# The head of an attention-and-Mish kernel reordered, one copy moved to ScalarE, and four output stores moved behind an activation

## The chip, the cores and the metric

One core of a Trainium2 chip runs the kernel. The metric is the device time of one execution in microseconds (us): the median of several runs, and for one of them a profile. The engines are PE (TensorE, matmuls), DVE (VectorE), ACT (ScalarE), POOL (GpSimd) and SP (SyncE, which only issues transfers here). ACT and POOL issue transfers as well, in line with their other work. The inputs are float32; the kernel works in float16 and accumulates in float32 in PSUM, the memory that PE writes and that DVE and ACT read.

## The reference

A causal linear attention with decay, per batch entry and head, and then two matrix products with an activation between them. B = 4, H = 8, S = 768, D = 64; w_in is 512 x 2048 and w_out 2048 x 512.

```python
Dmask = where(rel >= 0, lam ** rel, 0)           # within a block
for each block b of the sequence:
    intra = (einsum('bhic,bhjc->bhij', qb, kb) * Dmask) @ vb
    inter = einsum('bhid,bhde->bhie', qb * lam ** (pos + 1), kv_state)
    out[block] = intra + inter
    kv_state = lam ** block * kv_state + (kb * rev_pow)^T @ vb
x = out as (B*S) x (H*D)
h = x @ w_in
g = h * tanh(softplus(h))                        # Mish
result = g @ w_out
```

## The kernel before

The sequence is cut into NG = 6 groups n of C = 128 positions; with B = 4 batch entries a group has four chunks of 128 rows. Chunk c = 4 n + b is one batch entry's 128 positions, all eight heads. For the chunks of groups 0 and 1, one chunk goes through these steps:

- `first_t(c)` (L246): PE transposes k into PSUM tile `pk`, ACT copies it to `pkT` (L237); PE transposes q into `pq`, DVE copies it to `pqT` (L242 in group 0). In group 0 the q of chunks 1 to 3 is laid out differently, so its transposes are 16 small matmuls (L222).
- `first_s(c)` (L269): `scores` (L253) multiplies pkT and pqT on PE into two PSUM tiles `pS`, 8 matmuls (L260). `masks(c, 0)` and `masks(c, 1)` (L264) multiply each tile by the decay mask on DVE, giving two tiles `sb`.
- `first_o(c)` (L294): `outputs` (L274) multiplies sb with v into PSUM tile `pO` on PE; `copy_out` (L290) copies it on ACT into `xt`, the transposed attention output of the group. There is one PSUM buffer each for pk, pq and pO, so outputs of a chunk wait for copy_out of the chunk before.

Then the dense part: `mm1_unit(n, u)` (L424) is four matmuls of 512 columns (L421) that make 128 of the 2048 hidden columns in PSUM tile `ph` (two buffers), and one Mish on ACT into `hsg` (L428). `mm2_unit` multiplies hsg with w_out into `po` (L453); after the last part of a batch entry `mm2_out` (L460) copies po on ACT to `osb` (L462 calls L468) and issues the store on ACT's queue (L465). For later groups k and q are transposed by DMA (`turn`), and their scores and outputs are placed between the dense units.

The order of each engine's work is the order of the program text (a manual schedule); each engine runs its own instructions strictly in that order and waits on semaphores for the others. `busy(m)` (L172) issues m matmuls of zeros, 512 columns each, into a tile that nobody reads. `clear(b)` sets a part of the state `wst` to zero on DVE; `scale_k` (L301) makes `ktil`, the decayed k, on DVE for group 0 and on POOL for group 1. The loads of k, q, v and the weights are issued by POOL; w_in arrives in pieces, in this order: two of 128 columns, one of 256, three of 512 columns.

The program text around the change: the head is L492 to L538 (chunks 0 to 3, with `mm1_part` computing the first 384 columns of units 0 and 1 ahead of the last chunk). L557 to L568 run the 16 units of group 0 and place chunk 4's and 5's steps behind units 11 to 15. The loop at L584 runs the rest: for n = 1 the output units of groups 0 and 1, from n = 2 on the 16 units of group n and its output units.

Of the kernel before, what the change touches and what calls it, by code (L numbers as in the profile page):

```python
# [9 lines left out]
AF = mybir.ActivationFunctionType  # L10
# [3 lines left out]
def bc(ap, axis, n):  # L14
    shape = list(ap.shape)
    shape.insert(axis, n)
    return ap.unsqueeze(axis).broadcast_to(shape)
# [3 lines left out]
def kernel(  # L21
# [10 lines left out]
    nc = tc.nc  # L32
    B, H, S, D = q.shape
    C = 128
    NG = S // C
# [136 lines left out]
    def busy(m):  # L172

        t = ps.tile([128, 4 * C], F32, name="busy", tag="ph", bufs=2)
        for _ in range(m):
            nc.tensor.matmul(t, kzero, kzero2, start=True, stop=True)  # L176
# [38 lines left out]
    def turn_pe(c, name):  # L215

        src = (k0 if c == 0 else kn[c] if c < B else ktil[c]) if name == "pk" else (q0 if c == 0 else qn[c])
        if 0 < c < B and name == "pq":
            pt = ps.tile([128, JP, C], F32, name=name, tag=name)
            for r in range(RS):  # L220
                for x in range(2):
                    nc.tensor.matmul(  # L222
                        pt[64 * x : 64 * x + 64].rearrange("p j (s r) -> p j s r", r=RS)[:, :, :, r],
                        src[:, r, :], own[:, :, x, :], start=True, stop=True)
        else:
            pt = ps.tile([128, JP, C], F16, name=name, tag=name)
            for j in range(JP):
                nc.tensor.matmul(  # L228
                    pt[:, j, :], src[:, 2 * j : 2 * j + 2, :].rearrange("p h c -> p (h c)"), ident,
                    is_transpose=True, start=(j == 0), stop=(j == JP - 1),  # L230
                )
        kq[c, name] = work.tile([128, JP, C], F16, name=f"{name}T", tag=f"{name}T", bufs=2)
        return kq[c, name], pt

    def first_k(c):
        to, pt = turn_pe(c, "pk")
        nc.scalar.activation(to, pt, AF.Copy)  # L237

    def first_q(c):
        to, pt = turn_pe(c, "pq")  # L240
        if c < B:
            nc.vector.tensor_copy(to, pt)  # L242
        else:
            nc.vector.tensor_tensor(out=to, in0=pt, in1=lq, op=ALU.mult)

    def first_t(c):  # L246
        first_k(c)
        first_q(c)
# [4 lines left out]
    def scores(c):  # L253

        kT, qT = kq[c, "pk"], kq[c, "pq"]
        pS = [ps.tile([128, JP, C], F32, name="pS", tag=("pS", "po")[t], bufs=1 + t) for t in range(2)]
        for j in range(JP):
            for t in range(2):
                rs = slice(64 * t, 64 * t + 64)
                nc.tensor.matmul(pS[t][:, j, :], kT[rs, j, :], qT[rs, j, :], start=True, stop=True)  # L260
        score[c] = pS
        sb0[c] = [None, None]

    def masks(c, t):  # L264
        sb0[c][t] = work.tile([128, JP, C], F16, name="sb", tag="sb", bufs=4)
        nc.vector.tensor_tensor(out=sb0[c][t], in0=score[c][t],  # L266
                                in1=dm[:, t] if c < B else bc(maskT, 1, JP), op=ALU.mult)

    def first_s(c):  # L269
        scores(c)  # L270
        masks(c, 0)
        masks(c, 1)

    def outputs(c):  # L274
        n, b = divmod(c, B)
        if xt[n] is None:
            xt[n] = work.tile([128, JP, GT], F16, name="xt", tag="xt", bufs=2)
        psO = ps.tile([128, JP, C], F32, name="pO", tag="pO")
        vf = vz[c].rearrange("p h c -> p (h c)")
        for j in range(JP):  # L280
            if n:
                nc.tensor.matmul(psO[:, j, :], wst[:, b, j, :],
                                 kq[c, "pq"][:, j, :], start=True, stop=False)
            for t in range(2):
                o = 4 * D * j + D * t
                nc.tensor.matmul(psO[:, j, :], vf[:, o : o + 128], sb0[c][t][:, j, :],  # L286
                                 start=(n == 0 and t == 0), stop=(t == 1))
        outs[c] = psO

    def copy_out(c):  # L290
        n, b = divmod(c, B)
        nc.scalar.activation(xt[n][:, :, b * C : (b + 1) * C], outs[c], AF.Copy)  # L292

    def first_o(c):  # L294
        outputs(c)
        copy_out(c)
# [4 lines left out]
    def scale_k(i):  # L301

        t = work.tile([128, H, D], F16, name="ktil", tag="ktil", bufs=8)
        (nc.vector if i < B or i >= (NG - 1) * B else nc.gpsimd).tensor_tensor(  # L304
            out=t, in0=kn[i], in1=bc(lk, 2, D), op=ALU.mult)
        ktil[i] = t
# [101 lines left out]
    def behind(src):  # L408
        nc.gpsimd.tensor_copy(tick, src)  # L409
# [46 lines left out]
                )  # L456

    last_out = [None]

    def mm2_out(n, b, po, lo, hi, copy, queue):  # L460
        osb = work.tile([128, hi - lo], F32, name="osb", tag=f"osb{hi - lo}", bufs=3)
        copy(osb, po[:, lo:hi])  # L462
        last_out[0] = osb
        r0 = b * S + n * C
        queue.dma_start(out=out[r0 : r0 + C, lo:hi], in_=osb)  # L465

    def act_copy(o, i):
        nc.scalar.activation(o, i, AF.Copy)  # L468
# [20 lines left out]
    def clear(b):  # L489
        nc.vector.memset(wst[:, b], 0.0)  # L490
# [14 lines left out]
    nc.scalar.activation(lbc, lnp, AF.Exp, scale=float(C))  # L505
    q_decays()
    busy(1)
    scores(0)
    masks(0, 0)
    first_t(1)  # L510
    masks(0, 1)
    nc.scalar.preload_act_table(AF.Mish)
    busy(1)
    scores(1)
    masks(1, 0)
    outputs(0)
    first_t(2)
    copy_out(0)
    masks(1, 1)
    busy(2)  # L520
    first_s(2)
    first_o(1)
    clear(1)
    busy(2)
    first_t(3)
    clear(2)
    busy(2)
    first_s(3)
    first_o(2)
    busy(2)  # L530
    mm1_part(0, 0, 0, GT - C)
    first_o(3)
    mm1_part(0, 1, 0, GT - C)
    scale_k(0)
    scale_k(1)
    clear(3)
    scale_k(2)
    scale_k(3)  # L538
# [15 lines left out]
    load_wout(3)  # L554
    load_k(2 * B)
    load_q(2 * B)
    steps = {11: ((first_t, 4),), 13: ((first_s, 4),), 14: ((first_t, 5),), 15: ((first_o, 4), (first_s, 5))}  # L557
    for u in range(NKI):
        mm1_unit(0, u)
        if u in (1, 3):  # L560
# [9 lines left out]
    for c in (g + 1, g + 2, g + 3):  # L570
        load_k(c)
        load_q(c)
    steps = {(4, 0): ((first_t, 6),), (4, 1): ((first_o, 5), (first_s, 6)), (4, 2): ((first_t, 7),),
             (4, 3): ((first_o, 6), (first_s, 7)), (5, 1): ((first_o, 7),),
             (6, 1): ((state_half, 0), (turn, g)), (6, 2): ((state_half, 1),)}
# [8 lines left out]
    for n in range(NT - 1, NG):  # L584
        dense = [(mm2_unit, m, b, part) for m in ((0, 1) if n < NT else (n,))
                 for b in range(B) for part in range(WS)]
        if n >= NT:
            dense = [(mm1_unit, n, ni) for ni in range(NKI)] + dense
        todo = {}

        def at(u, f, *args):
            todo.setdefault(u, []).append((f, args))

        if n + 1 < NG:
            pairs = []
            for b in (0, 2):
                s = Pair()
                s.n, s.b = n + 1, b
                pairs.append(s)
            steps = (((9, pair_s, 0), (13, pair_o, 0), (16, pair_s, 1), (20, pair_o, 1),  # L600
                      (24, pair_a, 1)) if n < NT else
                     ((4, pair_s, 0), (8, pair_o, 0), (13, pair_s, 1), (17, pair_o, 1),
                      (20, pair_a, 1)))
            for u, f, b in steps:
                at(u, f, pairs[b])
        if n == NT:
            at(0, lambda: behind(hsg[n][0:1, 0, 0:1]))
            at(0, turn, (n + 1) * B + 2)
            at(0, turn, (n + 1) * B + 3)
        if n + 2 < NG:  # L610
            c = (n + 2) * B
            loads_ = [(f, c + b) for b in range(B) for f in (load_k, load_q)]
            loads_ += [(load_v, c + b) for b in range(B)]
            for x, (f, i) in enumerate(loads_):
                if n >= NT:
                    u = (1, 2, 3, 5, 6, 8, 10, 11, 12, 13, 14, 15)[x]
                    at(u, lambda u=u: behind(hsg[n][0:1, u, 0:1]))
                else:
                    u = 7 + x // 2 * 4
                    if x % 2 == 0:  # L620
                        at(u, lambda: behind(last_out[0][0:1, 0:1]))
                at(u, f, i)
            for b, u in enumerate((21, 23) if n < NT else (18, 19, 21, 23)):
                at(u, turn, c + b)
        for u, (fn, *args) in enumerate(dense):
            fn(*args)
            for f2, args in todo.get(u, ()):
                if args and isinstance(args[0], Pair):
                    args[0].spare = "po" if u < NKI - 1 and n >= NT else "ph"
                f2(*args)  # L630
# [30 lines left out]
```

## Time and profile before

| | |
|---|---|
| median of 3 runs | 211.84 us (211.42 to 212.21) |
| the profiled execution | 212.23 us, of which 210.4 us span from the first to the last instruction |
| PE busy | 204.0 us, 97% of the span |
| ACT busy | 86.5 us, 41% |
| DVE busy | 68.3 us, 32% |
| POOL busy | 98.8 us, 47% |
| L453 (second product) | 400 matmuls, 85.4 us |
| L421 (first product) | 328 matmuls, 73.2 us |
| L176 (`busy`) | 16 matmuls, 6.8 us |

How to read it: busy time counts a matmul from its start to its modelled end, and neighbours overlap, so 97% does not mean that PE does useful work all that time; the filler of L176 counts as busy too. A timeline row gives the start, the time from the first start to the last end of a run of like instructions, the engine (with a q where its sequencer issues a transfer), line, operation, output and inputs, shapes, the count, and in brackets the idle time of the engine before it and what ended it.

### The profile page before, as it was taken

Reading aid. Unit: us, or ns where it says so; the run is one execution under the profiler, and the core shown is the slowest. Engines: PE = TensorE matmul, PEld = TensorE weight load, DVE = VectorE, ACT = ScalarE, POOL = GpSimd, SP = SyncE. Lnnn points to the kernel's source line nnn. Section 1 sums busy time; section 2 is a strip of 40 time slices with the busy share of each in tenths; the row PEclk is TensorE's granted clock in tenths of the full one; section 3 lists DMA queues with packets and bytes.
Section 4 is the critical chain, followed back from the end, with each engine's and each line's share of the span. In section 5 each row is a group of like instructions: output and inputs, shape, how many; then the busy total and the mean of one; then the engine's idle time right before and its main releaser. Section 6 shows DMA issues by size and latency. Waiting matters only on the chain.

```text
span 210.4 us, 4359 instructions
## 1 busy us (share of the span) xinstructions
PE 204.0 (97%) x1794; PEld 111.0 (53%) x1794; DVE 68.3 (32%) x124; ACT 86.5 (41%) x150; POOL 98.8 (47%) x143
## 2 busy tenths in 40 slices
PE   7998999999999999999999999999999999999993
PEld 4556446999745554454544445544455544444452
DVE  7578715525004632042540042681042600000000
ACT  4944576665421112356312456212456221666120
POOL 7997299934964558796874176840000000000000
PEclk9999999999999999999999999999999999999999
DMA  8999999999999999999996799996802042100112
GB/s 123 146 166 200 182 152 98 189 188 158 135 181 189 196 131 170 204 169 151 134 152 161 197 78 94 138 160 149 189 3 50 2 103 101 50 0 0 53 50 100
DMA packets 107591, 26.78 MB, mean 127 GB/s; under 512 B 99890, under 2 KB 104626, under 8 KB 107570
## 3 DMA queue, kind: packets, MB, share of 16 engines
q0 software_dynamic: 75776, 13.38, 83.1%
q1 hardware_dynamic: 27296, 6.63, 20.8%
q10 hardware_dynamic: 4498, 6.49, 10.0%
q8 instruction: 14, 0.23, 0.5%
q14 instruction: 7, 0.06, 0.1%
HBM read 27.26 MB, written 6.29 MB: 159 GB/s over the span
## 4 chain that ended last, share of the span: by engine, by line
PE 94%; DMA 2%; DVE 1%; ACT 1%; issue 0%
PE po L453 40%; PE ph L421 34%; PE ph L439 7%; PE pS L365 2%; PE pO L286 2%; PE pO L392 2%; DMA kn<-in_k_dram 2%; PE pv L329 1%; PE pS L260 1%; DVE pqT L242 1%; PE pk L228 1%; PE pq L222 1%; PE pO L371 1%; PE pq L228 1%; PE busy L176 1%; ACT xt L292 1%
## 5 line engine op out<-in xcount | busy, mean ns | idle before, releaser
L453 PE MATMUL po<-wout,hsg 128*128 128x512 f16 (+2 forms) x400 | 85.4, 371 | 0.0
L421 PE MATMUL ph<-xt,win 128*128 128x512 f16 (+2 forms) x328 | 73.2, 374 | 0.4 <-ACT xt L292 0.3
L453 PEld LDWEIGHTS <-hsg 128*128 128x128 f16 x400 | 37.7, 98 | 42.4
L428 ACT ACTIVATE hsg<-ph 128x512 f16<-128x512 f32 x80 | 47.7, 597 | 29.8 <-PE ph L421 29.5
L421 PEld LDWEIGHTS <-win 128*128 128x128 f16 x328 | 30.8, 98 | 36.0 <-issue 2.0
L468 ACT ACTIVATE osb<-po 128x512 f32<-128x512 f32 (+1 forms) x24 | 14.2, 593 | 74.1 <-PE po L453 56.4
L380 DVE TENSOR_TENSOR sb<-pS,maskT 128x512 f16<-128x512 f32 x32 | 19.9, 682 | 57.8 <-PE pS L365 57.8
L70 POOL DMA_DIRECT2D kn<-in_k_dram x23 | 21.0, 912 | 6.9 <-issue 2.3
L88 POOL DMA_DIRECT2D vz<-in_v_dram x24 | 21.7, 906 | 2.6 <-DMA win<-in_moe_w_in_dram 1.5
L85 POOL DMA_DIRECT2D qn<-in_q_dram x20 | 18.0, 898 | 5.5 <-DMA wout<-in_moe_w_out_dram 4.2
L304 POOL TENSOR_TENSOR ktil<-kn,lk 128x512 f16<-128x512 f16 x16 | 16.6, 1048 | 2.6 <-ACT hsg L428 2.4
L439 PE MATMUL ph<-xt,win 128*128 128x128 f16 x256 | 15.6, 219 | 0.4 <-ACT xt L292 0.4
L398 DVE TENSOR_TENSOR xtok<-pO,lqt 128x512 f16<-128x512 f32 x16 | 10.3, 685 | 15.8 <-PE pO L392 15.8
L439 PEld LDWEIGHTS <-win 128*128 128x128 f16 x256 | 14.5, 98 | 0.7 <-issue 0.3
L462 DVE COPY osb<-po 128x128 f32<-128x128 f32 x1 | 0.3, 292 | 38.7 <-PE po L453 38.7
L443 ACT ACTIVATE hsg<-ph 128x512 f16<-128x512 f32 x16 | 9.6, 597 | 7.3 <-PE ph L439 7.3
L345 POOL TENSOR_TENSOR wc<-raws,lbc 128x512 f16<-128x512 f32 x8 | 8.6, 1095 | 5.2 <-DVE raws L344 5.2
L409 POOL COPY tick<-hsg 1x1 f16<-1x1 f16 x25 | 4.4, 176 | 12.0 <-ACT hsg L428 12.0
L176 PE MATMUL busy<-kzero 128*128 128x512 f16 x16 | 6.8, 503 | 1.2 <-DVE kzero L158 1.2
L266 DVE TENSOR_TENSOR sb<-pS,maskT 128x512 f16<-128x512 f32 x8 | 5.1, 685 | 4.9 <-PE pS L260 4.9
L292 ACT ACTIVATE xt<-pO 128x512 f16<-128x512 f32 x8 | 4.8, 596 | 4.6 <-PE pO L286 4.4
L304 DVE TENSOR_TENSOR ktil<-kn,lk 128x512 f16<-128x512 f16 (+1 forms) x8 | 6.4, 838 | 0.0
(75 smaller groups left out, 120.5 us busy)
## 6 DMA issues: line engine op xcount, KB each, us to landing
out_dram<-osb ACTq DMA_DIRECT2D x23, 256.0 KB, 2.9
vz<-in_v_dram POOLq DMA_DIRECT2D x24, 128.0 KB, 4.9
kn<-in_k_dram POOLq DMA_DIRECT2D x23, 128.0 KB, 5.2
qn<-in_q_dram POOLq DMA_DIRECT2D x23, 128.0 KB, 5.2
wout<-in_moe_w_out_dram POOLq DMA_DIRECT2D x4, 512.0 KB, 9.3
win<-in_moe_w_in_dram POOLq DMA_DIRECT2D x3, 512.0 KB, 9.7
kn<-in_k_dram SPq DMA_DIRECT2D x1, 256.0 KB, 3.4
qn<-in_q_dram ACTq DMA_DIRECT2D x1, 256.0 KB, 4.1
```

Of the source, the lines that this page charges most:

```text
L70: nc.gpsimd.dma_start(out=kn[i], in_=chunk_rows(k, i))
L85: nc.gpsimd.dma_start(out=qn[i], in_=chunk_rows(q, i))
L88: nc.gpsimd.dma_start(out=vz[i % NVB][:, :, 0:D], in_=chunk_rows(v, i))
L304: (nc.vector if i < B or i >= (NG - 1) * B else nc.gpsimd).tensor_tensor(out=t, in0=kn[i], in1=bc(lk, 2, D), op=ALU.mult)
L380: nc.vector.tensor_tensor(out=s.sb[x][t], in0=pS[x][t], in1=bc(maskT, 1, JP), op=ALU.mult)
L398: nc.vector.tensor_tensor(out=xtok[:, :, :, t, :], in0=s.pO[t], in1=bc(bc(lqj[:, :, t], 1, 2), 3, D), op=ALU.mult)
L421: nc.tensor.matmul(ph_t[ni][:, lo:hi], win_t(ni, kc), xt[n][:, kc, lo:hi], start=(kc == 0), stop=(kc == NKC - 1))
L428: nc.scalar.activation(hsg[n][:, ni, :], ph_t.pop(ni), AF.Mish)
L439: nc.tensor.matmul(ph[:, u, :], win_t(w * s + u, kc), xt[n][:, kc, b * C : (b + 1) * C], start=(kc == 0), stop=(kc == NKC - 1),)
L443: nc.scalar.activation(hsg[n][:, w * s : w * s + w, b * C : (b + 1) * C], ph, AF.Mish)
L453: nc.tensor.matmul(po[:, lo:hi], hsg[n][:, ki, b * C : (b + 1) * C], wout[part][:, kk, lo:hi], start=(ki == 0), stop=(ki == NKI - 1),)
L468: nc.scalar.activation(o, i, AF.Copy)
```

## The change

Five things change in the text.

1. In the head, the masks of chunk 0 and of chunk 1 are taken together, directly behind their scores, and `outputs(0)` stands ahead of the scores of chunk 1, `first_o(2)` ahead of the scores of chunk 3.
2. Four of the nine `busy` matmuls from L513 on go, and the memsets of `wst` move: `clear(2)` behind the first two `scale_k`.
3. The copy of q^T of chunk 2 is made by ACT instead of DVE.
4. `first_o(4)` moves from behind unit 15 of group 0 to behind unit 14.
5. The store of the last batch entry of groups 1 to 4 is issued behind the Mish of the next group's first unit instead of ahead of it.

```diff
     def first_q(c):
         to, pt = turn_pe(c, "pq")
-        if c < B:
+        if c == 2:
+            nc.scalar.activation(to, pt, AF.Copy)
+        elif c < B:
             nc.vector.tensor_copy(to, pt)
...
     last_out = [None]
+    late = []
...
-        queue.dma_start(out=out[r0 : r0 + C, lo:hi], in_=osb)
+        late.append(lambda: queue.dma_start(out=out[r0 : r0 + C, lo:hi], in_=osb))
+        if b < B - 1 or n in (0, NG - 1):
+            late.pop()()
...
     busy(1)
-    scores(0)
-    masks(0, 0)
+    first_s(0)
     first_t(1)
-    masks(0, 1)
     nc.scalar.preload_act_table(AF.Mish)
-    busy(1)
-    scores(1)
-    masks(1, 0)
     outputs(0)
+    first_s(1)
     first_t(2)
     copy_out(0)
-    masks(1, 1)
     busy(2)
     first_s(2)
     first_o(1)
+    first_t(3)
     clear(1)
-    busy(2)
-    first_t(3)
-    clear(2)
-    busy(2)
+    busy(1)
+    first_o(2)
     first_s(3)
-    first_o(2)
     busy(2)
     mm1_part(0, 0, 0, GT - C)
     first_o(3)
     mm1_part(0, 1, 0, GT - C)
     scale_k(0)
     scale_k(1)
+    clear(2)
     clear(3)
...
-    steps = {11: ((first_t, 4),), 13: ((first_s, 4),), 14: ((first_t, 5),), 15: ((first_o, 4), (first_s, 5))}
+    steps = {11: ((first_t, 4),), 13: ((first_s, 4),), 14: ((first_t, 5), (first_o, 4)), 15: ((first_s, 5),)}
...
             fn(*args)
+            if u == 0 and late:
+                late.pop()()
```

DVE's instructions in the head, chunk 0 to the first scaled k, before (a row is line, operation, output and inputs, shape of a partition block, and the count of like rows):

```order
L242 COPY pqT<-pq 128x512
L490 MEMSET wst 128x256
L266 TENSOR_TENSOR sb<-pS,dm 128x512
L242 CAST pqT<-pq 128x512
L266 TENSOR_TENSOR sb<-pS,dm 128x512 x2
L242 CAST pqT<-pq 128x512
L266 TENSOR_TENSOR sb<-pS,dm 128x512 x3
L490 MEMSET wst 128x256
L242 CAST pqT<-pq 128x512
L490 MEMSET wst 128x256
L266 TENSOR_TENSOR sb<-pS,dm 128x512 x2
```

The same stretch of DVE now (the lines of the new text are two to five higher):

```order
L244 COPY pqT<-pq 128x512
L495 MEMSET wst 128x256
L268 TENSOR_TENSOR sb<-pS,dm 128x512 x2
L244 CAST pqT<-pq 128x512
L268 TENSOR_TENSOR sb<-pS,dm 128x512 x4
L244 CAST pqT<-pq 128x512
L495 MEMSET wst 128x256
L268 TENSOR_TENSOR sb<-pS,dm 128x512 x2
```

Both masks of chunk 0 now stand ahead of the cast of chunk 1; the cast of chunk 2 is gone, and the four masks of chunks 1 and 2 follow each other.

ACT's instructions from the copy of chunk 1's k^T to the end of group 0, before:

```order
L237 ACTIVATE pkT<-pk 128x512
L512 ACT_TABLE_LOAD
L237 ACTIVATE pkT<-pk 128x512
L292 ACTIVATE xt<-pO 128x4x128 x2
L237 ACTIVATE pkT<-pk 128x512
L292 ACTIVATE xt<-pO 128x4x128 x2
L428 ACTIVATE hsg<-ph 128x512 x12
L237 ACTIVATE pkT<-pk 128x512
L428 ACTIVATE hsg<-ph 128x512 x3
L237 ACTIVATE pkT<-pk 128x512
L428 ACTIVATE hsg<-ph 128x512
L292 ACTIVATE xt<-pO 128x4x128
```

And now:

```order
L237 ACTIVATE pkT<-pk 128x512
L515 ACT_TABLE_LOAD
L237 ACTIVATE pkT<-pk 128x512
L242 ACTIVATE pqT<-pq 128x512
L294 ACTIVATE xt<-pO 128x4x128 x2
L237 ACTIVATE pkT<-pk 128x512
L294 ACTIVATE xt<-pO 128x4x128 x2
L430 ACTIVATE hsg<-ph 128x512 x12
L237 ACTIVATE pkT<-pk 128x512
L430 ACTIVATE hsg<-ph 128x512 x3
L237 ACTIVATE pkT<-pk 128x512
L294 ACTIVATE xt<-pO 128x4x128
```

The copy of chunk 2's q^T has come in behind that of its k^T and ahead of the copy of outputs(0); at the end, the copy of outputs(4) stands ahead of the last Mish (L430, the next row) instead of behind it.

ACT at the end of group 1's output units and the start of group 2, before:

```order
L468 ACTIVATE osb<-po 128x512
L465 DMA out_dram<-osb 128x512
L468 ACTIVATE osb<-po 128x512
L465 DMA out_dram<-osb 128x512
L428 ACTIVATE hsg<-ph 128x512 x16
```

And now:

```order
L473 ACTIVATE osb<-po 128x512
L468 DMA out_dram<-osb 128x512
L473 ACTIVATE osb<-po 128x512
L430 ACTIVATE hsg<-ph 128x512
L468 DMA out_dram<-osb 128x512
L430 ACTIVATE hsg<-ph 128x512 x15
```

The last store of the group has changed places with the first Mish of the next.

## The prediction

> **What bounds the kernel now.** I read the page first, its chain of waits above all, then the timelines of single engines where that chain leaves TensorE (PE).
>
> ```profile
> span 210.4 us, 4359 instructions
> PE 94%; DMA 2%; DVE 1%; ACT 1%; issue 0%
> ```
>
> Nearly the whole chain is PE. So a microsecond is saved only where PE now waits or runs filler ahead of real work, and what it saves shifts everything behind it. Both happen in the head, where the `busy` matmuls (L176) fill waits without producing anything. PE's timeline there:
>
> ```profile
> 8.35 1.06 PE L222 MATMUL pq<-ident,qn 128*64 128x64 f16 x16
> 9.34 0.61 PE L176 MATMUL busy<-kzero 128*128 128x512 f16 x1
> 10.19 0.40 PE L260 MATMUL pS<-pqT,pkT 64*128 64x128 f16 x8 [0.24 <-DVE pqT L242]
> 10.53 0.82 PE L286 MATMUL pO<-sb,vz 128*128 128x128 f16 x8
> 11.18 0.39 PE L228 MATMUL pk<-ident,kn 128*128 128x128 f16 x4
> 11.50 0.64 PE L222 MATMUL pq<-ident,qn 128*64 128x64 f16 x16
> 12.07 0.60 PE L176 MATMUL busy<-kzero 128*128 128x512 f16 x2
> ...
> 16.08 0.40 PE L260 MATMUL pS<-pqT,pkT 64*128 64x128 f16 x8 [0.25 <-DVE pqT L242]
> ...
> 17.72 0.81 PE L421 MATMUL ph<-xt,win 128*128 128x384 f16 x4 [0.25 <-ACT xt L292]
> 18.36 0.61 PE L286 MATMUL pO<-sb,vz 128*128 128x128 f16 x8
> 18.81 1.46 PE L421 MATMUL ph<-xt,win 128*128 128x384 f16 x12
> ```
>
> Columns are start, time, instruction, count. The reader should see a loop of dependent steps per chunk (transposes pk and pq, copy pqT, scores pS, masks sb, outputs pO, copy xt) with filler in its gaps. The partners are VectorE (DVE) and ScalarE (ACT):
>
> ```profile
> 7.96 0.69 DVE L266 TENSOR_TENSOR sb<-pS,dm 128x512 f16<-128x512 f32 x1 [0.47 <-PE pS L260]
> 9.45 0.69 DVE L242 CAST pqT<-pq 128x512 f16<-128x512 f32 x1 [0.80 <-PE pq L222]
> 10.06 1.28 DVE L266 TENSOR_TENSOR sb<-pS,dm 128x512 f16<-128x512 f32 x2
> 16.50 1.29 DVE L266 TENSOR_TENSOR sb<-pS,dm 128x512 f16<-128x512 f32 x2 [0.20 <-PE pS L260]
> ```
>
> ```profile
> 11.66 0.60 ACT L237 ACTIVATE pkT<-pk 128x512 f16<-128x512 f16 x1 [1.31 <-PE pk L228]
> 12.16 0.59 ACT L292 ACTIVATE xt<-pO 128x512 f16<-128x512 f32 x1
> 19.01 0.60 ACT L292 ACTIVATE xt<-pO 128x512 f16<-128x512 f32 x1 [1.34 <-PE pO L286]
> ```
>
> From these rows come the steps I use. PE to DVE takes 0.04 (pq ends 9.41, cast starts 9.45). DVE or ACT to PE takes 0.05 (cast ends 10.14, pS starts 10.19). Two ACT copies start 0.50 apart, two masks 0.60. On PE, starts follow each other by 0.34 (pS to the next group), 0.45 (pO to the next, 18.36 to 18.81), 0.32 (pk to pq) and 0.57 (pq to the next). Early matmuls are slower: pq takes 1.06 at 8.35 but 0.64 at 11.50.
>
> **Head, replayed in the new order.** DVE masks chunk 0 twice at once: 7.96 + 0.60 + 0.69 = 9.25, before pq(1) ends at 9.41, so the mask hides. Outputs(0) takes the filler's place at 9.34. I give it twice the warm 0.45, an estimate from the two pq rows, so it ends its slot at 10.24. Scores(1) start there, against 10.19 before: nothing gained yet. But outputs(0) and its wait no longer stand behind them. Pk(2) starts at 10.58 (was 11.18), pq(2) at 10.90, ending 11.54.
>
> Now ACT copies q^T of chunk 2. Its price is a row of the same shape, L292: 0.60. ACT starts pkT at 11.06 (pk's end plus 0.09, as from 11.57 to 11.66), pqT at 11.58 (pq's end plus 0.04), done 12.18; copy_out(0) follows at 12.08 and ends 12.68. Left on DVE, the copy would stand behind the second mask of chunk 1 (started at 10.66 + 0.60) and be done at 11.86 + 0.69 = 12.55; on ACT it is sooner, but delays copy_out(0), and outputs(1) need that PSUM bank. So outputs(1) start at 12.73, pk(3) at 13.18, pq(3) at 13.50 ending 14.14, DVE's cast ends 14.87, scores(3) start at 14.92 (was 16.08). In between copy_out(1) ends at 13.99; outputs(2) run from 14.29 behind one filler, and xt(2) is ready near 15.55. Behind two fillers of 0.22 (two matmuls of that shape differ from one by that much, below) the first ph piece starts at 15.69 (was 17.72: 2.03 earlier).
>
> What is late next is the mask of chunk 3: scores(3) plus 0.42 plus 1.29 = 16.63. Outputs(3), from 16.33 otherwise, hang on it: the second matmul waits to 16.68, and the next ph piece starts at 17.07 (16.68 plus seven of eight slots of 0.056). It was 18.81. Copy_out(3) keeps its 0.20 behind that piece (19.01), and the units follow it, so all moves by the same. **Head: 1.74 us earlier.** The moved memsets of wst lie in DVE's waits; if they did not, each is one 0.27 DVE piece that the state matmuls, over 2 us later, would see. Four of nine fillers go; they are part of this replay, not a further gain.
>
> **Outputs(4) ahead of the last unit of group 0.**
>
> ```profile
> 32.54 1.29 DVE L266 TENSOR_TENSOR sb<-pS,maskT 128x512 f16<-128x512 f32 x2 [1.29 <-PE pS L260]
> 33.53 0.39 PE L228 MATMUL pq<-ident,qn 128*128 128x128 f16 x4
> 36.14 0.55 PE L439 MATMUL ph<-xt,win 128*128 128x128 f16 x7 [0.35 <-ACT xt L292]
> ```
>
> PE waits 0.35 for the copy of outputs(4). In the new order unit 15 runs while ACT copies (0.60, against a unit of four 0.22 plus scores of 0.34), so that wait goes. Outputs(4) now follow pq(5), 33.53 + 0.22 = 33.75; their third matmul needs the mask that ends at 33.83, plus 0.05: some 0.06 to 0.1 of new wait. **Net 0.28.** Bounds: 0 to 0.35.
>
> **The store behind Mish.** Four boundaries between groups, from 86 us on. Rows: the two matmuls around the start of the third unit at each, an undisturbed pair, the first matmul of the unit ahead, and ACT:
>
> ```profile
> 87.74 0.77 PE L421 MATMUL ph<-xt,win 128*128 128x512 f16 x2
> 119.00 0.73 PE L421 MATMUL ph<-xt,win 128*128 128x512 f16 x2
> 150.21 0.78 PE L421 MATMUL ph<-xt,win 128*128 128x512 f16 x2
> 180.74 0.78 PE L421 MATMUL ph<-xt,win 128*128 128x512 f16 x2
> 32.88 0.59 PE L421 MATMUL ph<-xt,win 128*128 128x512 f16 x2
> 86.23 0.38 PE L421 MATMUL ph<-xt,win 128*128 128x512 f16 x1
> 86.48 0.60 ACT L468 ACTIVATE osb<-po 128x512 f32<-128x512 f32 x1 [2.86 <-PE po L453]
> 87.11 0.34 ACTq L465 DMA_DIRECT2D out_dram<-osb  x1
> 87.50 1.26 ACT L428 ACTIVATE hsg<-ph 128x512 f16<-128x512 f32 x2 [0.41 <-PE ph L421]
> out_dram<-osb ACTq DMA_DIRECT2D x23, 256.0 KB, 2.9
> ```
>
> A pair takes 0.59, here 0.77, 0.73, 0.78, 0.78: PE loses 0.18 + 0.14 + 0.19 + 0.19 = 0.70, because the third unit's buffer waits for a Mish that stood behind the store's issue. Without that issue ahead, Mish starts 0.04 after its unit (86.23 + 3 x 0.215 + 0.38 = 87.26), at 87.30 instead of 87.50, and is done at 87.90: the third unit goes on time at 87.96. The issue (0.34) then stands ahead of the second Mish, whose unit ends at 88.12. No row shows an issue behind an activation that it does not depend on. If it runs beside Mish, nothing is lost: 0.70. If it waits for the full end, it runs 87.93 to 88.27, the second Mish 88.32 to 88.92, and the fourth unit (due 88.82) loses about 0.14 each time: 0.14 in all. Nearest row: two ACT copies overlap by 0.1, so the issue ends at 88.14 and the second Mish starts almost when it did. I take **0.60**. The store itself lands 2.9 after its issue, now 0.7 later; its buffer is needed again sixteen units on, so nobody waits for it.
>
> **Sum.** 1.74 + 0.28 + 0.60 = 2.62 us off the profiled execution, 212.23 (210.4 of span and 1.8 around it): 209.6. That execution is 0.39 above the median of 211.84, to which the same saving applies: **209.2**.
>
> **What must not be late.** What arrives by DMA does not move with PE:
>
> ```profile
> 10.22 2.29 POOL L101 DMA_DIRECT2D win<-in_moe_w_in_dram  x3
> win<-in_moe_w_in_dram POOLq DMA_DIRECT2D x1, 128.0 KB, 4.7
> 26.38 1.04 POOL L304 TENSOR_TENSOR ktil<-kn,lk 128x512 f16<-128x512 f16 x1 [2.38 <-ACT hsg L428]
> 29.84 0.39 PE L228 MATMUL pk<-ident,ktil 128*128 128x128 f16 x4
> 62.45 1.30 SPq L313 DMA_TRANSPOSE kraw<-ktil  x1
> kraw<-ktil SPq DMA_TRANSPOSE x1, 5.8
> 71.29 0.62 PE L365 MATMUL pS<-qraw,kraw 64*128 64x128 f16 x16
> ```
>
> The first w_in piece lands at 14.92, needed at 15.69: 0.77 left. Ktil of chunk 4 is done at 27.42, needed at 29.84 - 1.74 = 28.10: 0.68 left. The last kraw of group 2 lands at 68.25, needed at 71.29 - 2.02 = 69.27: 1.02 left. All suffice, none by much.
>
> **Rivals.** (1) *Transfers become the bound.* Stores and reads now meet 2 us earlier; a transfer 1 to 3 us later than its row eats the margin and then stalls PE by 0 to 2. It speaks for it that the margins are under those shifts, against it that later loads and transposes are released by work that shifts too. Middle 1 lost: 210.2. Chance 0.16.
>
> (2) *PE speeds up later.* The granted clock reads full speed throughout, but the pq rows (1.06, then 0.64) show PE 1.66 times as fast after some point near 10 us. Were that to come only behind outputs(1), near 13.2, the starts from scores(1) to there (0.34 + 0.32 + 0.57 + 0.34 + 0.45 = 2.02) would take 1.66 times as long, 1.3 more: 210.5. Against: PE's work up to 10 us hardly thins. Chance 0.05. The Trainium skill ("TensorE: Matmul & The Clock Gate", The HAM clock gate) says that the clock doubles after a busy window of about 3.4 us which runs freely; by it the next change after 10 us would be near 13.4 and the time the same 210.5, and two executions of one kernel could differ by as much. Whether the doubling is that gate's, no row of before tells, since the clock column does not show it.
>
> (3) *Slower: PE falls back to the slow rate.* Place: 12 to 18 us, where fillers go and PE's waits grow. Slow work costs 0.66 more of its length, so over 2.62 / 0.66 = 4.0 us of dense work must run slow to turn the gain round; 5.5 us of it gives +1.0: 212.8. Against: the longest single wait in my replay is 0.4 (outputs(3)), and before has waits of 0.25 there without any such fall. Chance 0.03. The same page (Why this matters for your kernels) asks for an idle gap of over about 3 us before that happens; no row of before holds such a gap, so no row tests it.
>
> (4) *The head does not move*, because something I count as hidden, such as ACT's extra copy, stands in the loop again: the other two parts alone give 0.9, 211.0. Chance 0.04.
>
> **Chances and range.** Forecast 0.72 (208.6 to 209.9: the stores between 0.14 and 0.70, outputs(4) between 0 and 0.35, the head within 0.4). A measurement here tells about 0.5% from no change, 1.06 us: faster below 210.8. Forecast, most of (1) and half of (2) lie there: 0.87; the rest of them and (4) within: 0.09; slower 0.04. The range leaves out a little on the low side and (3), (4) and the far ends of (1) and (2): 208.5 to 210.7.
>
> **What would show it.** Right: the first 384-column ph piece near 15.7 and the second near 17.1; outputs(3) ending a wait for sb; no PE wait before L439's first matmul; pairs of 0.59 to 0.62 at the four boundaries, and no new gap at the fourth unit. Wrong: a gap before a ph, pk or pS matmul ended by a DMA, or 128-row matmuls still slow after 11 us.

## The result, and the profile after

| | before | after |
|---|---|---|
| median, 15 runs each | 211.97 us (211.40 to 213.12) | 210.38 us (209.33 to 213.40) |
| the profiled execution | 212.23 us, span 210.4 | 210.82 us, span 209.0 |

The ratio is 0.9921, with a 95% interval of 0.9898 to 0.9944: faster by 0.8%. Ratios, here and below, compare only the executions that lie within 1.5% of their kernel's fastest, so they need not be the quotient of the medians. The forecast was 209.2, the range 208.5 to 210.7. The sign and the range held; the change gave 1.6 us where 2.6 were forecast. The page of after tells where to look first: its span and the chain that ended last.

```profile
span 209.0 us, 4353 instructions
PE 65%; POOL 15%; DMA 15%; issue 2%; SPq 1%; DVE 0%; POOLq 0%
PE po L455 33%; PE ph L423 27%; DMA kn<-in_k_dram 6%; DMA wout<-in_moe_w_out_dram 5%; DMA kraw<-ktil 4%; POOL ktil L306 4%; POOL vz L88 3%; POOL kn L70 2%; PE pS L367 2%; PE pO L394 2%; SPq L315 1%; POOL qn L85 1%; POOL win L101 1%; POOL win L104 1%; POOL wc L347 1%
```

Before, PE was 94% of this chain. Now 30% of it is POOL and DMA: the kernel is no longer bound by PE alone. What PE waits for, longest in total first (us in total, times, longest):

```profile
PE busy L176 <- DVE kzero L158: 1.2, 1, 1.2
PE pS L367 <- DMA kraw<-ktil: 0.9, 1, 0.9
PE pk L228 <- POOL ktil L306: 0.5, 1, 0.5
PE pS L262 <- ACT pqT L242: 0.2, 1, 0.2
```

The first row is the start of the kernel and was there before. The second and third are new, and are the two late comers that the prediction named with margins of 1.02 and 0.68 us. PE's timeline at both places, and POOL's ktil and the load it waited for (KB and us from issue to landing):

```profile
28.32 0.40 PE L228 MATMUL pk<-ident,ktil 128*128 128x128 f16 x4 [0.49 <-POOL ktil L306]
...
70.70 0.40 PE L367 MATMUL pS<-qraw,kraw 64*128 64x128 f16 x8 [0.92 <-DMA kraw<-ktil]
```

```profile
27.22 1.04 POOL L306 TENSOR_TENSOR ktil<-kn,lk 128x512 f16<-128x512 f16 x1 [3.72 <-DMA kn<-in_k_dram]
```

```profile
kn<-in_k_dram POOLq DMA_DIRECT2D x1, 128.0 KB, 12.5
```

POOL sat idle for 3.72 us until kn of chunk 4 landed. In before the same load was issued at the same time, 14.62, took 11.6 us, and ktil ran from 26.38:

```profile
kn<-in_k_dram POOLq DMA_DIRECT2D x1, 128.0 KB, 11.6
```

Now the head of after on PE, to be read against the same groups of before:

```profile
8.19 0.64 PE L222 MATMUL pq<-ident,qn 128*64 128x64 f16 x16
8.80 0.90 PE L288 MATMUL pO<-sb,vz 128*128 128x128 f16 x8
9.75 0.40 PE L262 MATMUL pS<-pqT,pkT 64*128 64x128 f16 x8
...
11.82 0.40 PE L262 MATMUL pS<-pqT,pkT 64*128 64x128 f16 x8 [0.15 <-ACT pqT L242]
12.30 0.61 PE L288 MATMUL pO<-sb,vz 128*128 128x128 f16 x8
...
14.49 0.40 PE L262 MATMUL pS<-pqT,pkT 64*128 64x128 f16 x8
...
15.27 0.81 PE L423 MATMUL ph<-xt,win 128*128 128x384 f16 x4
15.91 0.89 PE L288 MATMUL pO<-sb,vz 128*128 128x128 f16 x8
16.64 1.46 PE L423 MATMUL ph<-xt,win 128*128 128x384 f16 x12
```

Every step stands in the order that the replay had, each some 0.4 earlier than replayed: the first ph piece at 15.27 (15.69), the second at 16.64 (17.07). The 0.4 is no merit of the change: pq of chunk 1 takes 0.64 here and took 1.06 in before, so PE had reached its fast rate earlier in this execution. Outputs(3) take 0.89 instead of 0.61, which is the wait for the mask that the prediction put there: DVE's masks end at 16.20, and with 0.05 to PE and seven slots of 0.056 the next piece follows at 16.64.

```profile
14.91 1.29 DVE L268 TENSOR_TENSOR sb<-pS,dm 128x512 f16<-128x512 f32 x2 [0.20 <-PE pS L262]
```

At a boundary between groups, ACT after:

```profile
86.49 0.60 ACT L430 ACTIVATE hsg<-ph 128x512 f16<-128x512 f32 x1 [0.22 <-PE ph L423]
86.55 0.34 ACTq L468 DMA_DIRECT2D out_dram<-osb  x1
87.35 0.60 ACT L430 ACTIVATE hsg<-ph 128x512 f16<-128x512 f32 x1 [0.27 <-PE ph L423]
```

The store's issue (ACTq, 86.55 to 86.89) runs while the Mish runs (86.49 to 87.09), and the second Mish waits only for PE. Nothing is lost at the fourth unit.

How far PE's work stands ahead of before, at the start of one group of matmuls each (from the timelines, taken before rounding, so a difference can be 0.01 off the starts shown; the last column is the best of the experiments below):

| place | before | after | ahead | with both transfers in time |
|---|---|---|---|---|
| pv, behind the head | 20.20 | 18.02 | 2.17 | 1.95 |
| pk of chunk 4 | 29.84 | 28.32 | 1.52 | 1.95 |
| pO of chunk 5 | 38.37 | 36.46 | 1.91 | 2.36 |
| pO of the second pair, group 2 | 75.54 | 74.73 | 0.81 | 2.36 |
| pS, group 3 | 90.83 | 89.83 | 0.99 | 2.54 |
| pS, group 4 | 122.03 | 120.91 | 1.12 | 2.67 |
| pS, group 5 | 153.29 | 152.03 | 1.26 | 2.81 |
| span | 210.4 | 209.0 | 1.4 | 2.9 |

Read down the column "ahead": the head gives 2.17, ktil takes 0.65, outputs(4) give 0.39, kraw takes 1.10, and the first three boundaries give 0.18, 0.13 and 0.14, the last about as much. Nothing else moves. (The losses are somewhat larger than the waits in the rows, 0.49 and 0.92: those count from the modelled end of the matmul before.) About 0.4 of the 2.17 is the earlier fast rate.

### The profile page after: what moved, and what is told of

It is laid out like the page before. It is cut to its first block, busy times and chain, and to the rows that moved or that the text cites. A ratio compares the mean times of both kernels' runs of the same rounds, so it can differ in the third digit from the quotient of the medians.

```text
span 209.0 us, 4353 instructions
## 1 busy us (share of the span) xinstructions
PE 202.3 (97%) x1790; PEld 110.1 (53%) x1790; DVE 67.8 (32%) x123; ACT 87.2 (42%) x151; POOL 98.7 (47%) x143
## 4 chain that ended last, share of the span: by engine, by line
PE 65%; POOL 15%; DMA 15%; issue 2%; SPq 1%; DVE 0%; POOLq 0%
PE po L455 33%; PE ph L423 27%; DMA kn<-in_k_dram 6%; DMA wout<-in_moe_w_out_dram 5%; DMA kraw<-ktil 4%; POOL ktil L306 4%; POOL vz L88 3%; POOL kn L70 2%; PE pS L367 2%; PE pO L394 2%; SPq L315 1%; POOL qn L85 1%; POOL win L101 1%; POOL win L104 1%; POOL wc L347 1%
## 5 line engine op out<-in xcount | busy, mean ns | idle before, releaser
L430 ACT ACTIVATE hsg<-ph 128x512 f16<-128x512 f32 x80 | 47.7, 597 | 29.5 <-PE ph L423 29.5
L411 POOL COPY tick<-hsg 1x1 f16<-1x1 f16 x25 | 4.4, 177 | 11.7 <-ACT hsg L430 11.6
L176 PE MATMUL busy<-kzero 128*128 128x512 f16 x12 | 5.4, 526 | 1.2 <-DVE kzero L158 1.2
L288 PE MATMUL pO<-sb,vz 128*128 128x128 f16 x64 | 5.9, 219 | 0.3
```

The costliest lines, as they stand in the source:

```text
L430: nc.scalar.activation(hsg[n][:, ni, :], ph_t.pop(ni), AF.Mish)
```

## The experiments

The theory: the three parts pay as replayed, and two transfers that do not move with PE take 1.75 us back. The rival: the head pays less than it seems, and the waits are chance. Twelve kernels ran in three groups, the first from the changed kernel again to both edits, the second from the head alone to the stores at their old place, the third the rest; kernels of a group share their runs of before, so medians of different groups are compared less surely.

**The changed kernel again.**

> The changed kernel again, as the reference point of this call. Theory (late transfers): PE gains about 2.2 us in the head, 0.4 at outputs(4) and 0.6 to 0.7 at the four boundaries, and gives back 0.3 to 1 us waiting for ktil of chunk 4 (about 28 us) and 0.5 to 1.5 us waiting for the last kraw of group 2 (about 70 us); time about 210.4. Rival (the head's gain is just smaller than it looks, and the two waits come by chance in one profile): no such waits in this profile, the same time.

Measured 210.64, ratio 0.9933 (0.9900 to 0.9966), with both waits in the profile, 0.73 for ktil and 0.97 for kraw. As the theory has it.

**k of chunk 4 earlier.**

```diff
     for s in range(WS):
+        if s == WS - 1:
+            load_k(B)
         load_win(s)
...
     for i in range(B, NVB - 2):
-        load_chunk(i)
+        if i > B:
+            load_k(i)
+        load_q(i)
+        load_v(i)
```

> Changed kernel, k of chunk 4 loaded ahead of the last w_in piece. Theory: the wait for ktil of chunk 4 goes (0.65 us in the profile of after), but the last kraw of group 2 is bound by transfers and does not come earlier, so PE waits longer there: time within 0.4 us of the changed kernel. Rival (each wait costs by itself): 0.6 us faster.

Measured 210.28, ratio 0.9904 (0.9868 to 0.9939); the profiled span is 208.1. The wait for ktil is gone, a wait of 0.81 for kraw is left. Kraw came sooner by about as much as PE: PE asks for it 0.74 earlier than in after (68.64 instead of 69.38) and goes on 0.85 earlier (69.85 instead of 70.70), against what I had expected; the interval does not tell 0.4 from 0.6 us, so the times decide nothing here.

**Loads of group 3 two units later.**

```diff
-                    u = 7 + x // 2 * 4
+                    u = 9 + x // 2 * 4
```

> Changed kernel, the loads for group 3 released two units (1.7 us) later. Theory (these loads and the stores, released earlier by the faster head, hold up the transposes of group 2): the last kraw lands about 1 to 2 us sooner than 70.7 and its wait (1.1 us) shrinks below 0.4: 0.7 to 1.1 us faster than the changed kernel. Rival (SP's own transposes, not the loads, set that landing): landing and time unchanged.

A miss in its making. These loads wait for the copy of the last output that stands ahead of them in the program, and at unit 9 that is still the one of unit 7: the first load is issued at 60.50, no later than in the other profiles (61.35 in after). What did move is their place among POOL's other work, and transposes of group 3 came late. PE in that profile, and the clock (the columns are stretch, length, PE's busy time and matmuls, the granted clock, DMA share, GB/s):

```profile
91.45 0.34 PE L367 MATMUL pS<-qraw,kraw 64*128 64x128 f16 x6 [2.30 <-DMA kraw<-ktil]
```

```profile
86.00:91.00 5.00, 3.15 (x22) 1.00 1.76 150
91.50:92.70 1.20, 1.20 (x28) 0.98 1.85 188
92.70:96.10 3.40, 3.40 (x10) 0.51 1.86 156
96.10:100.00 3.90, 3.90 (x33) 1.00 1.36 87
```

After a wait of 2.3 us the clock is at half for 3.4 us, and the mean clock of this execution is 0.992. Median 212.50; two more of the 12 executions have a mean clock as low (0.984 and 0.990), so the median is no measure of the edit. The ratio, 0.9950 (0.9915 to 0.9985), shows no gain over the changed kernel. The wait for the last kraw of group 2 is 0.59. As the edit does not move the loads, none of this speaks for or against the theory.

**Both edits.**

> Changed kernel with both edits. Theory: both waits gone, 1.0 to 1.75 us faster than the changed kernel, about 209.0 (the 209.2 that was forecast without late transfers). Rival (something else, such as later loads of group 3, becomes late): no more than 0.4 us faster.

Measured 211.07, ratio 0.9953 (0.9921 to 0.9985): not the 209.0 that the theory gave, and no faster than the changed kernel, as the rival has it. The second edit does not do its work, and the wait for kraw is 0.77. The expectation failed, and whether the loads hold up kraw was still open.

**The head alone; outputs(4) and the stores alone.** The first is the changed kernel with the stores' edit undone (the diff of the stores at their old place, below) and this line as before; the second is before with only those two parts of the change.

```diff
-    steps = {11: ((first_t, 4),), 13: ((first_s, 4),), 14: ((first_t, 5), (first_o, 4)), 15: ((first_s, 5),)}
+    steps = {11: ((first_t, 4),), 13: ((first_s, 4),), 14: ((first_t, 5),), 15: ((first_o, 4), (first_s, 5))}
```

> Only the head's new order (and the copy on ScalarE); outputs(4) and the stores as before. Theory (late transfers swallow what comes ahead of 70 us): PE's head is 1.7 to 2.2 us earlier; the wait for the last kraw near 71 us is about 0.4 us shorter than in the changed kernel, because outputs(4) bring PE there later, and the four boundaries keep their 0.7 us: about 211.1, faster than before by 0.9. Rival (the parts add): the changed kernel plus 0.4 plus 0.7, about 211.6.

> Only outputs(4) ahead of the last unit and the late stores; the head as before. Both theories: 0.35 + 0.7 us faster than before, about 211.0, with no wait for ktil or kraw, since PE is ahead of before by only 0.35 us at those places. If the store's issue behind Mish costs at the fourth unit: 0.5 us less.

The tail alone: 211.02, ratio 0.9969 (0.9938 to 0.9999), profiled span 209.2 against 210.4, and no wait for ktil or kraw. In that profile PE is ahead of before by 0.27 behind the unchanged head, 0.67 behind outputs(4) and 1.27 at the end: 0.40 and 0.60, the 1.0 us that both theories gave. The times agree less sharply: 1.06 us by the medians, 0.7 by the ratio. The head alone: 211.20, ratio 0.9967 (0.9932 to 1.0002), which includes no change. In its profile (an execution of 212.18, above that median) PE is 1.83 ahead behind the head and 0.03 at the second pair. Ktil takes 0.23 (it ends at 28.17 and pk of chunk 4 starts at 28.23), and the wait for kraw is longer than in the changed kernel, where I had expected a shorter:

```profile
71.48 0.29 PE L367 MATMUL pS<-qraw,kraw 64*128 64x128 f16 x4 [1.39 <-DMA kraw<-ktil]
```

So the landing is not a fixed point in time; it scatters, from 69.6 to 71.8 us over the profiles that have the wait.

**The copy of q^T back on VectorE.**

```diff
-        if c == 2:
-            nc.scalar.activation(to, pt, AF.Copy)
-        elif c < B:
+        if c < B:
             nc.vector.tensor_copy(to, pt)
```

> Changed kernel with q^T of chunk 2 copied by VectorE again. By the replay of the prediction the head ends about 0.2 us later. Theory (late transfers): that is swallowed by a wait for ktil that is 0.2 us shorter, time as the changed kernel. Rival (parts add): 0.2 us slower, too little to see in the time, but the position of the units behind the waits would move.

Measured 210.86, ratio 0.9953 (0.9924 to 0.9982), as the changed kernel. PE in its head:

```profile
12.54 0.40 PE L260 MATMUL pS<-pqT,pkT 64*128 64x128 f16 x8 [0.54 <-DVE pqT L242]
```

Scores(2) wait 0.54 for DVE instead of 0.15 for ACT. Behind the head pv starts at 18.60, 0.24 to 0.36 later than in the changed head at the same pace (the table below): the copy on ACT is worth that much in place. The interval does not tell 0.2 us from nothing, so whether a late transfer swallows it is not shown.

**The stores at their old place.**

```diff
-        late.append(lambda: queue.dma_start(out=out[r0 : r0 + C, lo:hi], in_=osb))
-        if b < B - 1 or n in (0, NG - 1):
-            late.pop()()
+        queue.dma_start(out=out[r0 : r0 + C, lo:hi], in_=osb)
```

> Changed kernel with the stores at their old place. Both theories: pairs of matmuls at the four boundaries take 0.73 to 0.78 us again, time 0.6 to 0.7 us above the changed kernel, about 211.1. A store issue that costs at the second Mish would make it less.

Measured 211.60, ratio 0.9993 (0.9963 to 1.0022), 1.0 us above the 210.64 of the changed kernel in the group before, where 0.6 to 0.7 were expected; the two ratios' intervals just meet. In the profile the boundaries give nothing: the first twenty matmuls of group 2's units take 4.66 us as in before (4.48 in after), and PE, 0.08 behind before at pS of group 3, is still 0.08 behind at group 4 and 0.14 at group 5. All that the head and outputs(4) gave is gone by then: the wait for the last kraw of group 2 is 1.47, the longest so far, that for ktil 0.60, and PE waits 0.61 for the first w_in piece, another of the three transfers that the prediction named. That these longer waits make up the rest of the 1.0 us is likely, but one profile does not show it for the median.

**k of chunk 4 earlier, and PE asks for the second pair one unit later.**

```diff
-            steps = (((9, pair_s, 0), (13, pair_o, 0), (16, pair_s, 1), (20, pair_o, 1),
+            steps = (((9, pair_s, 0), (13, pair_o, 0), (17, pair_s, 1), (20, pair_o, 1),
```

> Changed kernel with k of chunk 4 ahead of the last w_in piece, and the second pair's scores of group 2 one unit (0.86 us) later. Theory (late transfers): PE no longer waits for ktil, and waits for the last kraw by at most 0.2 us instead of 0.8 to 1.0; the span is 0.8 to 1.5 us shorter than the changed kernel's, time about 209.4. Rival (the next transfer behind is as late): a new wait behind 72 us takes it, time as the changed kernel.

Measured 209.48 (209.28 to 210.63, 6 runs), ratio 0.9900 (0.9875 to 0.9925). Its chain, what PE waits for, and PE at the two places:

```profile
PE 90%; ACT 0%; DVE 0%; issue 0%
```

```profile
PE busy L178 <- DVE kzero L160: 1.2, 1, 1.2
PE pS L264 <- ACT pqT L244: 0.2, 1, 0.2
```

```profile
27.88 0.39 PE L230 MATMUL pk<-ident,ktil 128*128 128x128 f16 x4
...
69.80 0.62 PE L369 MATMUL pS<-qraw,kraw 64*128 64x128 f16 x16
```

No wait is left at either, the chain is PE's again, and the last column of the table above is this run: all three parts arrive at the end. This is the outcome that tells the theory from the rival. The median lies under both kernels; against the changed kernel itself the intervals overlap, so by the times alone it is not shown to be faster than that one.

**k of chunk 4 earlier, and the loads of group 3 one output later.**

```diff
-                    u = 7 + x // 2 * 4
+                    u = 11 + x // 2 * 4
```

> Changed kernel with k of chunk 4 ahead of the last w_in piece, and the loads for group 3 released by the copy of the next output (unit 11 instead of 7, 3.5 us later). Theory a (these loads hold up the last kraw): it lands 1 us or more sooner than 69.8 and its wait is under 0.3. Theory b (stores and SP's own chain of transposes set it): landing and wait as in the run with k of chunk 4 alone (0.8). In both, transposes for group 3 may come late near 90 us; a wait over 1 us there makes it slower.

Measured 209.81, ratio 0.9908 (0.9880 to 0.9936). This time the edit does what it says. First after: the timeline with POOL's first load of group 3 and SP's issue of the last kraw, and that kraw's us from issue to landing. Then the same of this run, with PE's later wait:

```profile
61.35 0.88 POOL L70 DMA_DIRECT2D kn<-in_k_dram  x1
...
62.69 2.42 SPq L315 DMA_TRANSPOSE kraw<-ktil  x1
```

```profile
kraw<-ktil SPq DMA_TRANSPOSE x1, 8.0
```

```profile
61.09 1.47 SPq L317 DMA_TRANSPOSE kraw<-ktil  x1
...
65.20 0.88 POOL L70 DMA_DIRECT2D kn<-in_k_dram  x1
...
98.54 0.40 PE L369 MATMUL pS<-qraw,kraw 64*128 64x128 f16 x8 [0.68 <-DMA kraw<-ktil]
```

```profile
kraw<-ktil SPq DMA_TRANSPOSE x1, 6.5
```

With the loads out of its way kraw takes 6.5 us instead of 8.0 and lands at 67.6, and PE does not wait there. Its issue is 1.6 us earlier as well, but not because of this edit: the run with k of chunk 4 alone issued it at 61.29, and there it took 8.5. All 14 profiles sort the same way. In the four where POOL issues group 3's first load behind that kraw (before, the tail alone, the cures on before, and this run) it took 5.7 to 6.5 us; in the ten where the load goes first, 6.9 to 8.8. Theory a holds: the loads that a faster PE releases sooner hold up the transposes that PE needs next. Their delay comes back at 98.5 us, 0.68.

**Without the last five fillers.**

```diff
     copy_out(0)
-    busy(2)
     first_s(2)
...
     clear(1)
-    busy(1)
     first_o(2)
     first_s(3)
-    busy(2)
     mm1_part(0, 0, 0, GT - C)
```

> Changed kernel without the last five filler matmuls (those from chunk 2 on). If fillers keep PE at the fast rate in the head: matmuls between 12 and 18 us at the slow rate and the units of group 0 later by 1 us or more. If they do not matter: units up to 0.2 us earlier, which the wait for ktil swallows, time as the changed kernel.

Two of its four executions, the profiled one among them, have a mean granted clock of 0.992, so its median of 212.08 is no measure of the edit; the ratio of the other two is 0.9924 (0.9890 to 0.9958), as the changed kernel. The matmuls of the head run at the fast rate without fillers. Pv starts at 18.15, not earlier but somewhat later than in the changed kernel's two profiles (18.02 and 17.94); PE waits 0.69 for q^T of chunk 2 and 0.27 for the first w_in piece. The half clock comes elsewhere:

```profile
13.20 0.64 PE L222 MATMUL pq<-ident,qn 128*64 128x64 f16 x16
...
71.89 0.40 PE L367 MATMUL pS<-qraw,kraw 64*128 64x128 f16 x8 [2.65 <-DMA kraw<-ktil]
```

```profile
72.00:72.80 0.80, 0.80 (x26) 1.00 2.38 171
72.80:76.20 3.40, 3.40 (x10) 0.50 1.45 186
76.20:80.00 3.80, 3.80 (x32) 1.00 0.79 108
```

Behind a wait of 2.65 us for kraw, ten matmuls fill 3.4 us: about 1.7 us lost on top of the wait.

**The two cures on the kernel before.**

> The kernel before with the two edits of the run with k of chunk 4 early and the pair one unit later. Theory (these transfers are in time before the change): no gain, within 0.3 us of before. Rival (the edits are worth something by themselves): 0.5 us or more faster than before.

Measured 211.87, ratio 1.0009 (0.9976 to 1.0042): no gain, as the theory has it. The transfers were in time until the change moved PE ahead of them.

## Why the prediction was right, and where it was short

**The head: right, in mechanism and size.** Profiles differ in when PE becomes fast, so like has to be compared with like. In those where pq of chunk 1 takes 1.06 us in full or nearly so, pv starts at:

| head | profiles | pv starts |
|---|---|---|
| old order | before, tail alone, cures on before | 20.20, 19.93, 20.05 |
| new order | both edits, head alone, and the two with k of chunk 4 earlier that ran last | 18.36, 18.36, 18.24, 18.29 |
| new order, copy on VectorE | copy back on VectorE | 18.60 |

The means are 20.06 and 18.31 (each row within 0.27): 1.75 us, where the replay gave 1.74. The replay's two dear points are in the rows: the mask that outputs(3) wait for, and copy_out(0) ahead of outputs(1). Rival (2) did not come: pq of chunk 2 takes 0.64 in every profile. In some PE was fast earlier than in before, in none later, and that is worth about 0.4 us.

**Outputs(4): right.** 0.28 forecast, 0.39 and 0.41 measured: the wait of 0.35 is gone, and no new one for the mask shows.

**The stores: right in the sum, by another way.** 0.60 forecast, 0.18 + 0.13 + 0.14 at the first three and about 0.14 at the last measured, 0.59 together. The issue overlaps Mish wholly, not by the 0.1 that I took from two ACT copies; against that, two of the four boundaries keep a remainder of 0.05.

**The sum: short by what was put down as in time.** The step that failed is the sentence "All suffice, none by much" under "What must not be late": landing times of one execution were held against needs that moved by 2 us, as if the landings would stay. They came later. Kn of chunk 4 landed 12.5 us after its issue instead of 11.6, and ktil was late by 0.65. The last kraw was issued no sooner than in before (62.69 and 62.45) and landed 8.0 us after its issue instead of 5.8, so at 70.7 instead of 68.25, and PE lost 1.10. That is the prediction's own sign of being wrong, a gap before a pk or pS matmul that a transfer ends. The margin of the first w_in piece, 0.77, did not always hold either: PE waits 0.61 and 0.27 for it in two of the profiles.

This is rival (1), which had 0.16 and a middle price of 1.0, and gave 210.2; measured were 210.38. That the two lie so close is in part luck: the profile lost 1.75, and about 0.4 of that was made good by the earlier fast rate. The range held because it took in this rival; the forecast's own stretch, 208.6 to 209.9, missed. The rival should have been the likeliest case. That the margins were small stood in the text; that later loads are released by work that shifts too stood there as well, but as a reason against. It is one for it: the loads for group 3 start sooner with PE and get ahead of a transpose that moves less. The experiment with those loads one output later shows this; why kn of chunk 4 took 0.9 longer is open. The loss to ktil came and went from profile to profile (four of the seven profiles with the new head and the old load order have it, 0.23 to 0.89), while the wait for kraw was in all nine profiles with the new head, the old scores and no later loads.

**The slower rival had the wrong place.** PE does fall back to half its rate, but behind a late transfer at 72 or 91 us, not where fillers went; taking five more fillers out left the head fast. Two of the 15 executions of after (213.17 and 213.40) have a mean granted clock of 0.992. That is what one stretch of 3.4 us at half clock makes of 211 us, and none of the runs of before that were recorded with the experiments is below 0.997; but those two were not profiled, so this is argued and not shown.

## What to carry to other kernels

A gain at the start is worth what the tightest transfer behind it leaves: for each transfer that is not released by the engine that gets faster, set what the shift leaves of its margin against how far its landing can move, not against one landing time; here the same transpose took 5.7 to 8.8 us. Where too little is left, move the loads or the request for them in the same step; here, in the profile, a reordered load and a request one unit later brought back all that two waits had taken. Transfers that the faster engine releases come sooner too, and here they got in the way of one that did not.

## What had not been expected of the hardware

An ACT-queue store issue (0.34 us) ran entirely inside an independent activation (0.60 us), at all four boundaries of after. PE's waits of 2.30 and 2.65 us were each followed, about 1 us after work went on, by 3.4 us at a granted clock of 0.5; waits of 1.39 and 1.47 were not. The Trainium skill ("TensorE: Matmul & The Clock Gate", Why this matters for your kernels) warns of idle gaps of over about 3 us; here 2.3 were enough.
